# Softmax exponentials on VectorE: two bit passes and a product replaced by three shifted bit patterns, with the shifts on GpSimd

## The chip, the cores and the metric

One core of one Trainium2 chip runs the whole kernel. The metric is device time in microseconds (us). Five engines work side by side: TensorE (PE, matrix products into PSUM), VectorE (DVE), ScalarE (ACT), GpSimd (POOL) and SyncE (SP), which here issues the DMAs. Each runs its own queue of instructions in order, and semaphores tie them together. PSUM has eight banks of 128 x 512 fp32.

## The reference

Two thousand and forty-eight tokens of 640 features in bf16, 32 heads of 20 features, and a GLU of 1728 hidden features. Both halves read the same layer-normed input.

```python
x  = A_x                                          # 1 x 2048 x 640
xn = layernorm(x)
q, k, v = split_heads(xn @ A_wqkv, H=32, Dh=20)
p  = softmax((q @ k.T) * 20 ** -0.5)              # 2048 x 2048 for each head
s  = merge_heads(p @ v) @ A_wo
g  = silu((sigmoid(xn @ B_w_gate) * (xn @ B_w_up)) @ B_w_down)
out = x + s * g
```

There are 32 x 2048 x 2048 exponentials, and their number sets the scale of the kernel.

## The kernel before

**Blocks and jobs.** Heads are taken in 8 groups of 4 (`GH`), queries in 4 chunks of 512 (`QC`). A group and a chunk make a block; there are 32 (`NBLK`). In a block, a job is one head and one tile of 128 keys: a score matmul with 32 rows of contraction (line 860) writes one PSUM bank of 128 keys x 512 queries, an exponential turns it into bf16 weights, and PV matmuls (line 897) multiply the weights with the 21 columns of `vts` (one column of ones, 20 of V) and add into the block's bank `oacc`. A block has 64 jobs, the kernel 2048. Four score matmuls use the four row groups of PE side by side, four PV matmuls the four column groups. An upper bound of each query's scores is subtracted through an extra row of the operands, so that no second pass over the scores is needed.

**Two ways to an exponential.** ScalarE reads one or two banks and writes `exp` into a `pt` tile (line 80). VectorE takes the other way: line 1194 adds an offset to the scaled score and converts it to a 16-bit integer `iv`, whose bits, read as bf16, are 2 to the integer part times one plus the fraction. That is too coarse alone. So three passes over a set of four jobs (`passes`, lines 945, 948 and 951) make two slabs of `pb`: the power of two by itself, and `iv` times a mantissa correction; one PV matmul for each slab adds both into `oacc`. In `add_unit`, `k` tells which pass a PV unit came from.

**PSUM.** `scA` holds two slots of two banks for ScalarE's pairs. Three more banks, `bank[0]` to `bank[2]` (`bk` in the profile), are shared by VectorE's jobs, by all other matmul work and by a slot's third job. `oacc` is the eighth.

**The order of instructions** of PE, ScalarE and VectorE is written by a planner that runs while the program is built. It steps a clock in 0.02 us, keeps when each engine, bank and buffer comes free by assumed costs (`T_F`, `T_PV`, `T_IV`, `T_PASS`, `t_exp`), and issues the next instruction of an engine that is free. PE chooses between a fill ("F": up to two or three jobs for ScalarE and one for VectorE, lines 1279 to 1314), a round of PV ("PV") and other matmul work ("M"). Changing from one kind to another is charged `T_MODE`. A fill gives VectorE a job if a bank is free and VectorE is nearly idle (line 1283). It gives ScalarE a third job only if the bank with the slot's own number is free and not taken by that VectorE job:

```python
want = SLOT if flex[nfill % 2] <= now and d_bank != nfill % 2 else SLOT - 1
```

`claim_act` takes a head's key tiles from the front, `claim_dve` from the back. Buffers limit how far work can run ahead: three `iv`, three `pb`, three `pt` for pairs and seven for triples (`NPT, NPB, NIV`).

**Other work.** "M" items are the projections (`mk_k`, `mk_q`, `mk_ku`, `mk_qu`, `mk_v`), the GLU (`mk_gu`, `mk_down`) and the output projection (`mk_out`). They are spread over the blocks by `due()`. After a block, `norm_a` copies `oacc` out and sends its row of sums through DRAM; `norm_b`, some 6.5 us later, takes the reciprocal (line 920), broadcasts it through DRAM (line 925) and has GpSimd multiply (line 927, `on_bf`), from where SP stores into `oU` (line 935). GpSimd does little else in the middle of the kernel and is not planned there: its instructions stand in the order in which the program writes them.

Of the kernel before, what the change touches and what calls it, by code (L numbers as in the profile page):

```python
# [11 lines left out]
BF16 = mybir.dt.bfloat16  # L12
# [20 lines left out]
NPT, NPB, NIV = (3, 7), 3, 3  # L33

LOG2E = 1.4426950408889634
# [3 lines left out]
def _bits_offset():  # L39

    f = (np.arange(4096) + 0.5) / 4096
    k = float(np.mean(((1.0 + f) ** 2 / 2 + 129.0 / 128.0) / 2.0 ** f))
    return 128.0 * (127.0 - float(np.log2(k)))


B_OFF = _bits_offset()


@with_exitstack
def kernel(  # L50
# [49 lines left out]
    kTs = [persist.tile([P, S], BF16, name=f"kT{i}") for i in range(2)]  # L100
    vts = [persist.tile([P, TT, 2 * GH, VW], BF16, name=f"v{i}") for i in range(2)]
# [320 lines left out]
    T_PASS = (0.605, 0.605, 1.15)  # L422
# [8 lines left out]
    v_at = {}  # L431
    o_at = {}
# [172 lines left out]
    def mk_v(pr, tts, at):  # L605
        st = {}

        def alloc():
            st["ps"] = misc_ps()

        def mm(i, kd):
            nc.tensor.matmul(st["ps"][:, i * 2 * GC:(i + 1) * 2 * GC],  # L612
                             lhsT=xn_tok(tts[i], kd),
                             rhs=wvs[pr][:, kd, :], start=(kd == 0), stop=(kd == KD - 1))

        def done(t):
            for tt in tts:
                v_at[(pr, tt)] = t
        return Item([("PE", alloc, [(0.08, lambda i=i, kd=kd: mm(i, kd)) for i in range(len(tts)) for kd in range(KD)]),
                     ("DVE", 0.065 + 0.167 * len(tts), lambda: v_evac(st["ps"], pr, tts), "free", done)], at)  # L620
# [229 lines left out]
    def claim_dve(had):  # L850
        for b in range(base(), min(NBLK, base() + 2)):
            if q_at.get(b, 1e9) > now:
                return None
            if n_left[b] >= (D_LAST if b < NBLK - 1 else D_LAST_END):
                return take(b, max((j for j in range(GH) if left[b][j]),
                                   key=lambda j: (j not in had, len(left[b][j]), j)), -1)
        return None
# [14 lines left out]
    def add_unit(b, kt, j, src, k, ready, rel):  # L872
        if k != 0:
            pv_jobs[(b, j)] = pv_jobs.get((b, j), 0) + 1
        pv_q[j].append(dict(b=b, kt=kt, j=j, k=k, src=src, ready=ready, rel=rel))
        pv_units[b] += 1

    def pv_pick(j):
        for u in pv_q[j]:
            if u["b"] == pv_block[0] and u["ready"] <= now and v_at.get((u["b"] // NQC // 2, u["kt"]), 1e9) <= now:  # L880
                return u
        return None
# [4 lines left out]
    def pv_emit(us, end):  # L887
        for u in us:
            b, kt, j, k = u["b"], u["kt"], u["j"], u["k"]
            pr, go = divmod(b // NQC, 2)  # L890
            pv_q[j].remove(u)
            pv_units[b] -= 1
            first = not pv_started.get((b, j))
            pv_started[(b, j)] = True
            last = pv_jobs.get((b, j), 0) == TT and not any(x["b"] == b for x in pv_q[j])
            lhsT = vts[pr % 2][:, kt, go * GH + j, 0:DH + 1]
            nc.tensor.matmul(oacc[32 * j:32 * j + DH + 1, :], lhsT=lhsT, rhs=u["src"], start=first, stop=last,  # L897
                             tile_position=(0, 32 * j), skip_group_check=True)
            left, i = u["rel"]
            left[i][0] -= 1  # L900
            left[i][1] = max(left[i][1], end + PL)
# [15 lines left out]
    def norm_b(b, on, lt):  # L917
        g, c = divmod(b, NQC)
        rt = w2.tile([P, GH * QC // P], FP32, tag="rt", bufs=2, name="rt")
        nc.vector.reciprocal(out=rt, in_=lt)  # L920
        rd = dram.tile([GH, QC], FP32, name="rd", tag="rd")
        nc.sync.dma_start(out=rd.rearrange("j (i c) -> (j i) c", c=GH * QC // P), in_=rt)
        rl = w2.tile([P, QC], FP32, tag="rl", bufs=1, name="rl")
        for j in range(GH):
            nc.sync.dma_start(out=rl[32 * j:32 * j + 32, :], in_=rd[j:j + 1, :].broadcast_to((32, QC)))
        on_bf = w2.tile([P, QC], BF16, tag="on_bf", bufs=2, name="on_bf")
        nc.gpsimd.tensor_tensor(out=on_bf, in0=on, in1=rl, op=ALU.mult)  # L927
        for j in range(GH):
            f = g * GC + j * DH
            r = 32 * j + 1  # L930
            left = DH
            while left:
                t, o = divmod(f, P)
                m = min(left, P - o)
                nc.sync.dma_start(out=oU[o:o + m, t, c * QC:(c + 1) * QC], in_=on_bf[r:r + m, :])
                f += m
                r += m
                left -= m


    def passes(d, k):
        n = len(d["jobs"])
        iv, pb = d["iv"][:, 0:n, :], d["pb"][:, :, 0:n, :]
        if k == 0:
            nc.vector.tensor_scalar(out=pb[:, 0, :, :].bitcast(I16), in0=iv, scalar1=0x7F80, scalar2=1,  # L945
                                    op0=ALU.bitwise_and, op1=ALU.bitwise_or)
        elif k == 1:
            nc.vector.tensor_scalar(out=pb[:, 1, :, :].bitcast(I16), in0=iv, scalar1=0x007F, scalar2=0x3F00,  # L948
                                    op0=ALU.bitwise_and, op1=ALU.bitwise_or)
        else:  # L950
            nc.vector.tensor_tensor(out=pb[:, 1, :, :], in0=iv.bitcast(BF16), in1=pb[:, 1, :, :], op=ALU.mult)  # L951
# [86 lines left out]
    with tc.manual_schedule(engines={ENG.PE, ENG.Activation, ENG.DVE}):  # L1038
# [9 lines left out]
        free = {"PE": 0.0, "ACT": 0.0, "DVE": 0.0}  # L1048
# [6 lines left out]
        dve_pass = []  # L1055
        dve_last = None
# [30 lines left out]
        def run_item(it, eng):  # L1087
# [5 lines left out]
            if len(op) > 4:  # L1093
                op[4](end + EL)
# [4 lines left out]
        while chain or items or glu_items or any(it.i < len(it.ops) for it in active):  # L1099
# [3 lines left out]
            if bb > blk_loaded:  # L1103
                blk_loaded = bb
                g, c = divmod(bb, NQC)
                if c == 0 and g + 1 < PG:
                    spread_wst(g + 1, load_wst(g + 1))
# [25 lines left out]
            for eng in ("ACT", "DVE"):  # L1133
# [21 lines left out]
                if it is not None:  # L1155
# [3 lines left out]
                    continue  # L1159
                if eng == "ACT":  # L1160
                    s = slots[nexp % 2]
                    if nexp < nfill and s["a"] is not None and s["at"] <= now:
# [3 lines left out]
                        if buf_free(pt_left[w], NPT[w - 2]):  # L1166
                            pt = w2.tile([P, w, QC], BF16, tag=f"pt{w}", bufs=NPT[w - 2], name=f"pt{w}")
                            if m == SLOT:
                                flex[nexp % 2] = now + t_exp(1) + EL
                            if m == SLOT:  # L1170
                                exp_act(pt[:, 2, :], bank[nexp % 2])
# [11 lines left out]
                if tm is not None:  # L1183
                    timed.remove(tm)
                    norm_b(*tm[1:])
# [4 lines left out]
                pass_ok = dve_pass and (dve_pass[0]["k"] > 0 or buf_free(pb_left, NPB))  # L1190
                if iv_ok and not (dve_last == "iv" and pass_ok and now < dq[0][3] + SLACK):
                    dve_last = "iv"
# [6 lines left out]
                    d["n"] += 1  # L1199
                    if d["n"] == len(d["jobs"]) and d is not dcur:  # L1200
                        dve_pass.append(d)
                elif pass_ok:
                    dve_last = "pass"
                    d = dve_pass[0]
                    k = d["k"]
                    if k == 0:
                        d["pb"] = w2.tile([P, 2, GH, QC], BF16, tag="pb", bufs=NPB, name="pb")
                        pb_left.append([2 * len(d["jobs"]), 0.0])
                        d["rel"] = (pb_left, len(pb_left) - 1)
                    passes(d, k)  # L1210
                    d["k"] += 1
                    end = now + T_PASS[k]
                    free["DVE"] = end
                    if k != 1:
                        for x, (b, kt, j) in enumerate(d["jobs"]):
                            add_unit(b, kt, j, d["pb"][:, k // 2, x, :], k, end + EL, d["rel"])
                    if k == 2:
                        dve_pass.pop(0)
                        iv_left[d["i"]][:] = [0, end]

            if dcur is not None and claimed[0] == NJOB * NBLK:
                if dcur["n"] == len(dcur["jobs"]):
                    dve_pass.append(dcur)
# [9 lines left out]
            if free["PE"] <= now:  # L1233
# [10 lines left out]
                if cur is None:  # L1244
# [3 lines left out]
                    if m_it is None:  # L1248
                        behind = done < due() + LAG
                        for f in ((2,) if not behind and claimed[0] < NJOB * NBLK and not (FALL and not pv_ok and not can_f) else [(2, 1 - own, own), (2, own, 1 - own)][M_ORD]):  # L1250
# [18 lines left out]
                elif can_f and (margin < URGENT or (stay is None and not (flex[nfill % 2] <= now + WAIT3 and flex[nfill % 2] > now and margin > WAIT3))):  # L1269
# [9 lines left out]
                if nxt == "F":  # L1279
# [5 lines left out]
                    want = SLOT if flex[nfill % 2] <= now and d_bank != nfill % 2 else SLOT - 1  # L1285
# [11 lines left out]
                    if jobs or d_new is not None:  # L1297
                        for x, t in enumerate(jobs):
                            score_mm(scA[nfill % 2][:, x, :] if x < 2 else bank[nfill % 2], *t)
# [8 lines left out]
                        if jobs:  # L1308
                            s["a"], s["at"], s["ends"] = jobs, end + PL, 0.0
                            if len(jobs) == SLOT:  # L1310
                                flex[nfill % 2] = 1e9
# [46 lines left out]
        assert not items and not glu_items and not any(it.i < len(it.ops) for it in active)  # L1358
        for tm in timed:
            norm_b(*tm[1:])  # L1360
# [30 lines left out]
```

## Time and profile before

| | |
|---|---|
| median of 2 runs | 842.79 us (842.42 to 843.16) |
| span of the profiled execution | 839.8 us |
| around the span, against the median | 3.0 us |
| PE busy | 788.4 us, 94% |
| VectorE busy | 765.4 us, 91% |
| ScalarE busy | 796.0 us, 95% |
| GpSimd busy | 77.5 us, 9% |
| exponential jobs on VectorE / ScalarE | 471 / 1577 |
| PV matmuls from `pt` / from `pb` | 1577 / 942 |

All sums are made against the profiled execution. Busy time is the union of an engine's instructions. The granted clock of TensorE is at full speed until the last slice. The kernel has a first part of about 40 us (load, layer norm, first projections), a middle to about 803 us, in which scores are made throughout, and an end. A line of a group reads: source line, engine, operation, output <- inputs, shape and type, count | busy us, mean ns of one | idle time before it and what ended it.

### The profile page before, as it was taken

To read this page: it belongs to the slowest core of one execution; us is meant where nothing else is said; L and a number is where in the kernel's file an instruction comes from. 1 tells how busy PE (TensorE), PEld (TensorE's weight loads), DVE (VectorE), ACT (ScalarE), POOL (GpSimd) and SP (SyncE) were. 2 spreads that over 40 slices of the span, in tenths; PEclk is the share of its full clock that TensorE was granted. 3 is DMA by queue.
4 is the path that set the end of the run, shared out by engine and by line. 5 is a ranking of instruction groups with operands and counts; after the bars stand their busy time and mean duration, and the time that the engine had idled before them with its cause. 6 is when DMAs were issued, how large, how long until landed. Compare 5 with 4: busy or idle time off the path is not lost.

```text
span 839.8 us, 16932 instructions
## 1 busy us (share of the span) xinstructions
PE 788.4 (94%) x6354; PEld 278.5 (33%) x6411; DVE 765.4 (91%) x1194; ACT 796.0 (95%) x1003; POOL 77.5 (9%) x84
## 2 busy tenths in 40 slices
PE   4799999999999999999999999999999999999995
PEld 2432323333333323333333233333233322333342
DVE  7789899999899998998999999999998988999994
ACT  7799999999999999999999999999999999999970
POOL 5000000000000001000000000000000000002333
PEclk9999999999999999999999999999999999999998
DMA  5711212123222132213121232131311223111642
GB/s 154 205 51 50 60 51 49 47 57 82 72 62 63 43 85 69 68 44 82 52 61 53 68 85 67 45 92 49 109 65 46 66 71 78 28 47 57 193 147 91
DMA packets 92979, 62.21 MB, mean 74 GB/s; under 512 B 34648, under 2 KB 86408, under 8 KB 92896
## 3 DMA queue, kind: packets, MB, share of 16 engines
q1 hardware_dynamic: 92608, 60.79, 25.7%
q8 instruction: 50, 0.82, 0.4%
q10 hardware_dynamic: 288, 0.33, 0.1%
q14 instruction: 33, 0.27, 0.1%
HBM read 46.24 MB, written 12.39 MB: 70 GB/s over the span
## 4 chain that ended last, share of the span: by engine, by line
ACT 49%; PE 28%; DVE 13%; issue 6%; DMA 2%; SPq 1%; POOL 0%; POOLq 0%; ACTq 0%; DVEq 0%
ACT pt L80 44%; PE scA L860 8%; PE oacc L897 5%; DVE iv L1194 5%; PE bk L679 4%; PE bk L641 3%; ACT tnh L80 3%; DVE pb L951 2%; PE bk L765 2%; PE bk L504 2%; DVE pb L945 1%; DVE pb L948 1%; DMA ld<-on 1%; PE psk L140 1%; ACT td L80 1%
## 5 line engine op out<-in xcount | busy, mean ns | idle before, releaser
L80 ACT ACTIVATE pt<-scA 128x1024 bf16<-128x1024 f32 (+1 forms) x729 | 720.2, 1153 | 4.6 <-PE bk L860 2.9
L1194 DVE TENSOR_SCALAR iv<-bk 128x512 int16<-128x512 f32 x471 | 318.6, 682 | 31.7 <-PE bk L860 30.2
L860 PE MATMUL scA<-q,kT 32*128 32x512 bf16 x1448 | 282.6, 382 | 16.7 <-ACT pt L80 9.6
L860 PE MATMUL bk<-q,kT 32*128 32x512 bf16 x600 | 215.5, 383 | 2.0 <-DVE iv L1194 1.7
L897 PE MATMUL oacc<-pt,v 128*21 128x512 bf16 x1577 | 183.1, 382 | 0.6 <-ACT pt L80 0.3
L860 PEld LDWEIGHTS <-kT 32*128 32x128 bf16 x2048 | 88.7, 91 | 261.6 <-issue 246.8
L897 PE MATMUL oacc<-pb,v 128*21 128x512 bf16 x942 | 152.9, 382 | 1.8 <-DVE on L910 1.5
L951 DVE TENSOR_TENSOR pb<-iv,pb 128x2048 bf16<-128x2048 bf16 x118 | 146.8, 1244 | 0.8
L641 PE MATMUL bk<-xnT,wgu 128*128 128x512 bf16 x471 | 142.6, 383 | 3.6 <-issue 1.7
L927 POOL TENSOR_TENSOR on_bf<-on,rl 128x512 bf16<-128x512 f32 x30 | 43.3, 1443 | 692.7 <-DMA rl<-rd 326.0
L80 ACT ACTIVATE pt<-bk 128x512 bf16<-128x512 f32 x129 | 94.5, 733 | 4.0 <-PE bk L860 3.8
L945 DVE TENSOR_SCALAR pb<-iv 128x2048 int16<-128x2048 int16 x118 | 86.3, 731 | 2.5
L679 PE MATMUL bk<-wd,hT 128*128 128x320 bf16 x448 | 86.9, 302 | 1.2 <-DVE iv L1194 0.7
L948 DVE TENSOR_SCALAR pb<-iv 128x2048 int16<-128x2048 int16 x118 | 82.6, 700 | 0.0
L897 PEld LDWEIGHTS <-v 128*21 128x21 bf16 x2519 | 50.4, 90 | 92.2 <-issue 69.4
L641 PEld LDWEIGHTS <-wgu 128*128 128x128 bf16 x520 | 37.1, 97 | 66.2 <-issue 50.4
L679 PEld LDWEIGHTS <-hT 128*128 128x128 bf16 x448 | 34.4, 97 | 48.4 <-issue 39.4
L504 PE MATMUL bk<-xnT,wu 128*120 128x512 bf16 x160 | 49.3, 399 | 0.4 <-DVE iv L1194 0.3
L80 ACT ACTIVATE tnh<-bk 128x512 bf16<-128x512 f32 (+1 forms) x56 | 41.6, 742 | 0.1
L649 DVE SCALAR_TENSOR_TENSOR hT<-tnh,bk 128x512 bf16<-128x512 bf16 x52 | 35.3, 680 | 5.9 <-PE bk L641 5.2
L612 PE MATMUL bk<-wv,xnT 128*128 128x160 bf16 x280 | 29.2, 234 | 0.7 <-ACT pt L80 0.6
L612 PEld LDWEIGHTS <-xnT 128*128 128x128 bf16 x280 | 18.6, 98 | 14.4 <-issue 14.1
(116 smaller groups left out, 381.3 us busy)
## 6 DMA issues: line engine op xcount, KB each, us to landing
wgu<-in_B_w_gate_dram SPq DMA_DIRECT2D x24, 320.0 KB
wgu<-in_B_w_up_dram SPq DMA_DIRECT2D x24, 320.0 KB
rl<-rd SPq DMA_DIRECT2D x120, 64.0 KB
gq_dram<-gqs SPq DMA_DIRECT2D x32, 160.0 KB
xnT<-gq_dram SPq DMA_DIRECT2D x12, 320.0 KB
xt<-in_A_x_dram SPq DMA_DIRECT2D x16, 160.0 KB
wd<-in_B_w_down_dram SPq DMA_DIRECT2D x1, 2080.0 KB
oU<-on_bf SPq DMA_DIRECT2D x104, 20.0 KB
```

The lines of the kernel that those rows point to most:

```text
L80: return nc.scalar.add_instruction(mybir.InstActivation(func=func, name=nc.get_next_instruction_name(), engine=ENG.Activation, ins=[nc.sca ...
L504: nc.tensor.matmul(st["ps"][0:UC, :], lhsT=wus[u][:, kd, i, :], rhs=xnT[:, c, kd, :], start=(kd == 0), stop=(kd == KD - 1))
L612: nc.tensor.matmul(st["ps"][:, i * 2 * GC:(i + 1) * 2 * GC], lhsT=xn_tok(tts[i], kd), rhs=wvs[pr][:, kd, :], start=(kd == 0), stop=(kd == ...
L641: nc.tensor.matmul(st[key][0:fs, :], lhsT=w[:, i, kd, ko * P:ko * P + fs], rhs=xnT[:, c, kd, :], start=(kd == 0), stop=(kd == KD - 1))
L679: nc.tensor.matmul(st["ps"][:, 0:HD], lhsT=hT[0:fsz[kf], kf, t4 * P:(t4 + 1) * P], rhs=wd[0:fsz[kf], kf, h * HD:(h + 1) * HD], start=(kf = ...
L860: nc.tensor.matmul(dst, lhsT=kTs[(b // NQC) % 2][32 * j:32 * j + 32, kt * P:(kt + 1) * P], rhs=qts[b % 3][32 * j:32 * j + 32, :], start=Tr ...
L897: nc.tensor.matmul(oacc[32 * j:32 * j + DH + 1, :], lhsT=lhsT, rhs=u["src"], start=first, stop=last, tile_position=(0, 32 * j), skip_group ...
L927: nc.gpsimd.tensor_tensor(out=on_bf, in0=on, in1=rl, op=ALU.mult)
L945: nc.vector.tensor_scalar(out=pb[:, 0, :, :].bitcast(I16), in0=iv, scalar1=0x7F80, scalar2=1, op0=ALU.bitwise_and, op1=ALU.bitwise_or)
L948: nc.vector.tensor_scalar(out=pb[:, 1, :, :].bitcast(I16), in0=iv, scalar1=0x007F, scalar2=0x3F00, op0=ALU.bitwise_and, op1=ALU.bitwise_or)
L951: nc.vector.tensor_tensor(out=pb[:, 1, :, :], in0=iv.bitcast(BF16), in1=pb[:, 1, :, :], op=ALU.mult)
L1194: nc.vector.tensor_scalar(out=d["iv"][:, j, :], in0=bank[bk], scalar1=B_OFF, scalar2=0.0, op0=ALU.add, op1=ALU.max)
```

## The change

The exponential on VectorE becomes a sum of three bit patterns. `iv` itself is read as bf16 and goes straight to a PV matmul with V. Two more patterns, `iv` plus 43 and `iv` plus 85, are made by GpSimd (`shift`), each by an integer addition over a set of four jobs, and go to PV matmuls with copies of V that are scaled by 2 to the minus 43/128 and minus 85/128. The three linear interpolations have their kinks at different places, so that the ripple of their sum is small. The passes of VectorE are gone.

What follows from it: `vxs` holds the two scaled copies of V, written by GpSimd (`scale_v`) after each evacuation of V; they exist for key tiles 8 to 15 only (`KX = 8`), so `claim_dve` takes only those. There are two `pb` and two `pt` for pairs instead of three and three. A job on VectorE has three PV units, with `k` 0, 1 and 2 (`None` for ScalarE's). GpSimd is planned like the other engines: shifts, scalings and the product of the normalization (`norm_c`, 5.5 us after `norm_b` in the plan) stand in the order of their planned times. The preference between a conversion and a pass on VectorE (`SLACK`) has no more use there.

Besides, a slot's third job takes any of the three shared banks that is free, and remembers it (`s["third"]`).

```diff
-NPT, NPB, NIV = (3, 7), 3, 3
+MF = (2,)
+NPT, NPB, NIV = (2, 7), 2, 3
+KX = 8
+SHIFTS = (43, 85)
+V_SCALE = tuple(2.0 ** (-t / UNIT) for t in SHIFTS)
...
+    vxs = [[persist.tile([P, TT - KX, 2 * GH, VW], BF16, name=f"vx{k}{i}") for i in range(2)] for k in range(2)]
...
-    T_PASS = (0.605, 0.605, 1.15)
+    T_SHIFT, T_VX, T_DIV, GL = (0.15, 0.445), 0.60, 1.45, 0.25
...
             if n_left[b] >= (D_LAST if b < NBLK - 1 else D_LAST_END):
-                return take(b, max((j for j in range(GH) if left[b][j]),
-                                   key=lambda j: (j not in had, len(left[b][j]), j)), -1)
+                js = [j for j in range(GH) if left[b][j] and left[b][j][-1] >= KX]
+                if js:
+                    return take(b, max(js, key=lambda j: (j not in had, len(left[b][j]), j)), -1)
...
-            lhsT = vts[pr % 2][:, kt, go * GH + j, 0:DH + 1]
+            v, kv = (vxs[k - 1][pr % 2], kt - KX) if k else (vts[pr % 2], kt)
+            lhsT = v[:, kv, go * GH + j, 0:DH + 1]
...
-    def passes(d, k):
-        ...
+    def shift(d, k):
         n = len(d["jobs"])
+        nc.gpsimd.tensor_scalar(out=d["pb"][:, k, 0:n, :].bitcast(I16), in0=d["iv"][:, 0:n, :],
+                                scalar1=float(SHIFTS[k]), scalar2=None, op0=ALU.add)
+
+    def scale_v(pr, tts, k):
+        nc.gpsimd.tensor_scalar(out=vxs[k][pr % 2][:, tts[0] - KX:tts[-1] + 1 - KX, :, 0:1 + DH],
+                                in0=vts[pr % 2][:, tts[0]:tts[-1] + 1, :, 0:1 + DH],
+                                scalar1=V_SCALE[k], scalar2=None, op0=ALU.mult)
...
+                if eng == "POOL":
+                    ...
+                    elif pool_pass and pool_pass[0]["at"] <= now and (pool_pass[0]["k"] > 0 or buf_free(pb_left, NPB)):
+                        ...
+                        shift(d, k)
+                        end = now + T_SHIFT[0] + T_SHIFT[1] * n
+                        ...
+                            add_unit(b, kt, j, d["pb"][:, k, x, :], k + 1, end + GL, d["rel"])
...
                             if m == SLOT:
-                                flex[nexp % 2] = now + t_exp(1) + EL
-                            if m == SLOT:
-                                exp_act(pt[:, 2, :], bank[nexp % 2])
+                                flex[s["third"]] = now + t_exp(1) + EL
+                                exp_act(pt[:, 2, :], bank[s["third"]])
...
-                    norm_b(*tm[1:])
+                    args = norm_b(*tm[1:])
+                    pool_at.append((now + 5.5, T_DIV, lambda args=args: norm_c(*args)))
...
+                    iv_left[d["i"]][0] += 1
+                    add_unit(*d["jobs"][j], d["iv"][:, j, :].bitcast(BF16), 0, end + EL, (iv_left, d["i"]))
...
-                    want = SLOT if flex[nfill % 2] <= now and d_bank != nfill % 2 else SLOT - 1
+                    third = next((f for f in (0, 1, 2) if flex[f] <= now and f != d_bank), None)
+                    want = SLOT if third is not None else SLOT - 1
...
-                            score_mm(scA[nfill % 2][:, x, :] if x < 2 else bank[nfill % 2], *t)
+                            score_mm(scA[nfill % 2][:, x, :] if x < 2 else bank[third], *t)
```

## The prediction

> **What bounds the kernel now.** I read the busy shares first, then the long middle stretch alone (40 to 803 us, in which scores are made), then the costs of one step on each engine.
>
> ```profile
> PE 788.4 (94%) x6354; PEld 278.5 (33%) x6411; DVE 765.4 (91%) x1194; ACT 796.0 (95%) x1003; POOL 77.5 (9%) x84
> 40.00:803.00 763.00, 736.89 (x5959) 251.48 (x6006) 712.94 (x1084) 756.82 (x935) 51.80 (x40) 1.00 0.24 67
> ```
>
> The second line is the stretch: 763 us, then busy PE, weight loads, VectorE (DVE), ScalarE (ACT), GpSimd (POOL). ACT works 756.8 of 763 us; GpSimd 51.8. PE's figure is no measure, because a matmul's record is longer than its turn, so I count PE's turns from starts in the timeline:
>
> ```profile
> 404.36 0.39 PE L860 MATMUL scA<-q,kT 32*128 32x512 bf16 x2
> 404.69 0.58 PE L679 MATMUL bk<-wd,hT 128*128 128x320 bf16 x3
> 405.28 0.39 PE L860 MATMUL scA<-q,kT 32*128 32x512 bf16 x2
> 405.60 0.61 PE L897 MATMUL oacc<-pb,v 128*21 128x512 bf16 x6
> 406.36 0.39 PE L860 MATMUL scA<-q,kT 32*128 32x512 bf16 x2
> ```
>
> A fill of scores (up to four matmuls side by side) holds PE for 0.32 us (404.36 to 404.69). Three rounds of four PV matmuls take 0.76 (405.60 to 406.36). If every run of one kind pays the same 0.11 once, a 512-wide round is 0.213 to 0.217.
>
> ```profile
> 400.05 1.18 ACT L80 ACTIVATE pt<-scA 128x1024 bf16<-128x1024 f32 x1
> 400.95 0.60 ACT L80 ACTIVATE td<-bk 128x320 bf16<-128x320 f32 x1
> ...
> 408.65 0.57 ACT L80 ACTIVATE td<-bk 128x320 bf16<-128x320 f32 x1
> 408.97 0.74 ACT L80 ACTIVATE pt<-bk 128x512 bf16<-128x512 f32 x1
> ```
>
> ACT's turns by the same rule: 0.90 for a pair of score banks, 0.32 for a td; a single bank is 0.48 (399.57 to 400.05 in the same view). With 719 pairs, 139 singles: 647 + 67 = 714 us for 1577 exponential jobs, 0.453 each. The GLU's tanh and the rest (56 and 7 at 0.48, 32 at 0.32) are 40. Together 754: **ACT bounds the stretch, at 99%.**
>
> PE before: 729 fills x 0.32 = 233; 2519 PV matmuls, four to a round, 630 x 0.213 = 134; other matmuls by their weight loads (763 of 512 columns, 576 of 320, 280 of 160, at 0.213 and in proportion) 163 + 77 + 19 = 259; at least one switch back per fill, 729 x 0.107 = 78. Sum 704, 92% of 763. PE is second.
>
> **The change, part by part.**
>
> ```profile
> L1194 DVE TENSOR_SCALAR iv<-bk 128x512 int16<-128x512 f32 x471 | 318.6, 682 | 31.7 <-PE bk L860 30.2
> L951 DVE TENSOR_TENSOR pb<-iv,pb 128x2048 bf16<-128x2048 bf16 x117 | 145.4, 1242 | 0.8
> L945 DVE TENSOR_SCALAR pb<-iv 128x2048 int16<-128x2048 int16 x117 | 85.8, 733 | 2.5
> L948 DVE TENSOR_SCALAR pb<-iv 128x2048 int16<-128x2048 int16 x117 | 82.0, 701 | 0.0
> L126 POOL COPY wqk<-wst 128x800 bf16<-128x800 bf16 x2 | 1.9, 968 | 0.1
> L240 POOL MEMSET wqk<- 128x1280 bf16 x1 | 1.3, 1338 | 0.0
> L927 POOL TENSOR_TENSOR on_bf<-on,rl 128x512 bf16<-128x512 f32 x30 | 43.3, 1443 | 692.7 <-DMA rl<-rd 326.0
> ```
>
> (1) VectorE loses three passes per four jobs: 733 + 701 + 1242 ns by the rows, so 0.67 us a job, 118 sets, 315 us. It is not the bound, so this by itself saves nothing; it opens room for more VectorE jobs. A job then costs VectorE one row of 0.68 us instead of 1.35, and a fill lasts longer than that, so a fill can nearly always carry one. Now it is 471 jobs on 729 fills, 0.65 a fill.
>
> (2) Any free bank as third: now 129 of 729 fills have a third ACT job, since it must be the fill's own bank and the VectorE job often holds that. More thirds mean fewer fills, at 0.32 + 0.107 of PE each; ACT gains nothing from them (1.38 for three is 0.46 each).
>
> (3) I take 0.9 VectorE and 2.4 ACT jobs per fill: 2048 / 3.3 = 620 fills, 560 VectorE jobs, 1488 ACT jobs. ACT: 1488 x 0.453 + 40 = **714**, 40 less than now. The 0.9 lies between today's 0.65 and one; the 2.4 between today's 1577 / 729 = 2.16 and 3, kept low because three banks must serve the VectorE job, the third and the GLU.
>
> (4) PE: a VectorE job now has three PV matmuls instead of two. 1488 + 3 x 560 = 3168, 792 rounds, 169 us (+35). Fills 620 x 0.32 = 198 (-35), switches 66 (-12), the rest 259. Sum **692** against 704: the third bank pays for the third matmul.
>
> (5) GpSimd: two shifts of 128x2048 int16 per set, 140 sets, 280 shifts. No such row exists. From below the memset (1164 ns the faster of two, for 1280 columns) gives 1.86 us in proportion; from above the slower copy (1085 for 800, strided) 2.78. The copy is the nearest, one input and 16 bits; its faster one (852) gives 2.18, and I take 2.2: 616 us. The issue order is planned with 0.15 + 0.445 x 4 = 1.93 (541 us). Besides: 30 on_bf at 1.27 (38), 30 scalings of V of about 504 columns at the copy's rate (0.54; 16), 19 output additions at 0.9 (17): 71. Sum **687**, 612 by the plan. GpSimd has room in 735 us until a shift costs (735 - 71) / 280 = 2.37 us.
>
> The page "GPSIMD Engine Reference" of the Trainium skill (section 3.1, and the table of 4.1) speaks against moving elementwise work there: it calls VectorE about twice as fast, but names one-input work as roughly line rate. By its 1.03 cycles an element at 1.2 GHz a shift would be an estimated 1.76 us before dispatch, by its 2.6 cycles 4.4 us. The sum by the first would be 493 + 71 = 564, by the second 1232 + 71 = 1303; the memset and copy rows above lie near the first.
>
> The two engines disturb each other in this trace:
>
> ```profile
> L927 POOL TENSOR_TENSOR on_bf<-on,rl x30: 1262/1272/2170, 73.7 to 784.6; 128x512 bf16<-128x512 f32 x30
> L945 DVE TENSOR_SCALAR pb<-iv x118: 546/693/1742, 38.2 to 810.5; 128x2048 int16<-128x2048 int16 x117, 128x1536 int16<-128x1536 int16 x1
> ```
>
> (Minimum, median, maximum in ns.) on_bf grows from 1.27 to 2.17 us, and a pass from 0.69 to 1.74. The passes are what goes away; the VectorE instruction that stays at every job reads PSUM. "SBUF — State Buffer" (Who interferes with whom) explains such pairs as an exclusive lock, taken by VectorE in its two-port modes or with two SBUF inputs. By it 16 aq instructions (L547) could still each wait a shift, an estimated 16 x 2 us on an engine with slack; the sum on ACT would stay.
>
> (6) Waits and queues. on_bf goes into GpSimd's queue 5.5 us after the reciprocal. Its DMAs take about 5.0 (in the timeline the reciprocal is done at 411.25 and on_bf starts at 416.29), so it mostly finds its data; when late, shifts queue behind it, and PV behind those. On SP the 136 oU stores wait for on_bf already (61.6 us in 28 waits) and may wait two shifts more; what stands behind them there is q loaded two blocks ahead, so I cost it at nothing; without that lead a block would start up to 4.4 us late. The scalings of V sit before the block that needs them and cost nothing but GpSimd's time. A set is finished 4.4 us after its last iv instead of 2.4 (starts 0.60 + 0.60 + 1.13), covered by the pt buffers except at the end: +2. One pt pair and one pb fewer: part of the loss below.
>
> **The sum.** ACT 714, PE 692, GpSimd 612 to 687 now stand close together, so no engine will reach today's 99%; I take 97% for ACT: 714 / 0.97 = 736, 27 less than 763, and +2 at the end: -25. The profiled span is 839.8; with 3.0 outside it is the median of 842.8. Forecast **818 us**. With one job per fill on VectorE and 2.2 on ACT (640 fills) ACT falls to 687, but PE is 273 + 259 + 175 = 707; at 97% 729 (total 811), at 98% without a loss at the end 721 (800). So the forecast's own range is 800 to 826.
>
> **The rivals.**
> *PE or the banks take over.* Sums within 3% of each other rarely overlap fully. If PE gets no better than today's 92%, 692 / 0.92 = 752, total 834; with thirds that fail to come (2.16 a fill, 0.9: 669 fills) it is 286 + 259 + 172 = 717, at 94% 763, no change. For it: three banks. Against: PE's idle time now is largely ACT's doing. 835 us, chance 0.22.
> *GpSimd is too slow.* Order on PE is fixed, so a late shift stops PV, then fills, then ACT. It decides from 2.37 us a shift, and costs 28 us per 0.1 us beyond. The kernel is slower by 2% from (780 - 71) / 280 = 2.53. At 2.6: 728 + 71 = 799, +36, total 879. For it: the slower copy (2.78 in proportion), and a plan made with 1.93. Against: memset and the faster copy, and the passes that disturbed GpSimd are gone. Chance 0.24.
> *Not more jobs on VectorE.* If buffers (two pb, held through both shifts) keep it near 471, ACT keeps its 754: 843 us, chance 0.06.
>
> **How the numbers follow.** Forecast 0.48: faster by over 2%. Within 2%, about what a measurement of this kernel can tell from no change: 0.22 + 0.06 = 0.28. Slower: 0.24. The range runs from the forecast's low end, 800, up to where GpSimd at 2.56 us puts it, 868; about 0.2 is left outside, mostly above.
>
> **What would show it.** iv instructions 530 to 620 and three PV matmuls each; fills about 620 with over 250 thirds; a shift start to start at 1.9 to 2.3 us; GpSimd busy 75 to 90% of the middle; ACT still above 95% there; no rise of PE waits on pb. The forecast is wrong if iv stays near 471, if ACT drops below 92% with PE waiting for a shift, or if a shift takes over 2.4 us.

## The result and the profile after

The changed kernel takes 1507.18 us (1505.23 to 1509.13) against 842.79: the ratio is 1.789, 95% interval 1.782 to 1.797. The forecast was 818 us, with a range from 800 to 868. The busy shares of the profiled execution:

```profile
PE 1019.1 (68%) x6904; PEld 307.3 (20%) x6904; DVE 553.4 (37%) x852; ACT 828.0 (55%) x1079; POOL 1388.3 (92%) x355
```

The stretch in which scores are made now runs from 40 to about 1465 us. The columns are PE, weight loads, VectorE, ScalarE, GpSimd, then granted clock:

```profile
40.00:1465.00 1425.00, 971.12 (x6560) 281.03 (x6556) 510.59 (x755) 797.14 (x1020) 1352.58 (x310) 0.78 0.13 36
```

The last two numbers are the DMA share and GB/s. ScalarE has fallen from 99% to 56% of the stretch, and GpSimd is at 95%. It has become the bound, by one group (count | busy us, mean ns | idle before it):

```profile
L965 POOL TENSOR_SCALAR pb<-iv 128x2048 int16<-128x2048 int16 (+1 forms) x242 | 1287.8, 5345 | 67.1 <-DVE iv L1238 57.3
L85 ACT ACTIVATE pt<-scA 128x1024 bf16<-128x1024 f32 x638 | 639.8, 1034 | 164.8 <-PE bk L876 147.5
L1238 DVE TENSOR_SCALAR iv<-bk 128x512 int16<-128x512 f32 x482 | 333.8, 695 | 792.2 <-PE bk L876 776.4
L85 ACT ACTIVATE pt<-bk 128x512 bf16<-128x512 f32 x296 | 179.8, 607 | 461.4 <-PE bk L876 444.9
```

The first line is the whole result: 242 shifts of 5.35 us on average, 1288 us. The other three read as the prediction's counts: 638 fills, 296 single banks, and 482 VectorE jobs. The chain from the shift to the idle engines stands in the waits (total us, times, longest), first in the kernel before, then in the changed one:

```profile
DVE iv L1194 <- PE bk L860: 30.2, 59, 2.0
ACT pt L80 <- PE bk L860: 6.7, 11, 2.6
```

```profile
DVE iv L1238 <- PE bk L876: 776.4, 367, 13.3
ACT pt L85 <- PE bk L876: 592.4, 265, 12.7
...
PE oacc L915 <- POOL pb L965: 420.7, 163, 6.5
```

Read from the bottom: PV on PE stood 163 times for a shift, up to 6.5 us; before, PV waited for `pb` 0.3 us in all. PE's order is fixed by the program, so the fills behind that PV came late, and ScalarE and VectorE waited for scores. The granted clock of TensorE fell to 0.78 in the stretch, where it was 1.00 before. It came back to 1.00 when the waits went (first experiment of the next section), so it is read here as going with them, not as a cause; no run separates the two.

### The profile page after: what moved, and what is told of

The parts are those of the page before. It is cut to its first block, busy times and chain, and to the rows that moved or that the text cites. A ratio compares the mean times of both kernels' runs of the same rounds, so it can differ in the third digit from the quotient of the medians.

```text
span 1507.4 us, 18107 instructions
## 1 busy us (share of the span) xinstructions
PE 1019.1 (68%) x6904; PEld 307.3 (20%) x6904; DVE 553.4 (37%) x852; ACT 828.0 (55%) x1079; POOL 1388.3 (92%) x355
## 4 chain that ended last, share of the span: by engine, by line
POOL 31%; PE 9%; issue 8%; DMA 1%; DVE 1%; ACT 1%; SPq 1%; POOLq 0%; DVEq 0%; ACTq 0%
POOL pb L965 29%; PE oacc L915 2%; PE scA L876 2%; PE bk L694 1%; PE bk L780 1%; DMA rl<-rd 1%; ACT pt L85 1%; DVE iv L1238 1%; PE bk L656 1%; POOL vx L969 1%; POOL on_bf L949 1%; PE bk L511 0%; SPq L943 0%; POOL xnT L790 0%; DMA rd<-rt 0%
## 5 line engine op out<-in xcount | busy, mean ns | idle before, releaser
L965 POOL TENSOR_SCALAR pb<-iv 128x2048 int16<-128x2048 int16 (+1 forms) x242 | 1287.8, 5345 | 67.1 <-DVE iv L1238 57.3
L85 ACT ACTIVATE pt<-scA 128x1024 bf16<-128x1024 f32 x638 | 639.8, 1034 | 164.8 <-PE bk L876 147.5
L915 PE MATMUL oacc<-pb,vx 128*21 128x512 bf16 x964 | 198.5, 467 | 430.4 <-POOL pb L965 420.7
L85 ACT ACTIVATE pt<-bk 128x512 bf16<-128x512 f32 x296 | 179.8, 607 | 461.4 <-PE bk L876 444.9
L915 PE MATMUL oacc<-pt,v 128*21 128x512 bf16 x1566 | 266.6, 468 | 0.0
L876 PE MATMUL bk<-q,kT 32*128 32x512 bf16 x778 | 243.4, 465 | 18.4 <-DVE otmp L787 10.8
L656 PE MATMUL bk<-xnT,wgu 128*128 128x512 bf16 x520 | 176.4, 455 | 0.6 <-DVE iv L1238 0.2
L915 PE MATMUL oacc<-iv,v 128*21 128x512 bf16 x482 | 132.2, 443 | 4.4 <-DVE hT L664 4.2
L915 PEld LDWEIGHTS <-vx 128*21 128x21 bf16 x964 | 48.6, 94 | 333.5 <-issue 317.1
L969 POOL TENSOR_SCALAR vx<-v 128x504 bf16<-128x504 bf16 (+2 forms) x30 | 33.3, 1111 | 15.8 <-DVE v L195 14.1
```

What stands on the lines that cost most here:

```text
L85: return nc.scalar.add_instruction(mybir.InstActivation(func=func, name=nc.get_next_instruction_name(), engine=ENG.Activation, ins=[nc.sca ...
L656: nc.tensor.matmul(st[key][0:fs, :], lhsT=w[:, i, kd, ko * P:ko * P + fs], rhs=xnT[:, c, kd, :], start=(kd == 0), stop=(kd == KD - 1))
L876: nc.tensor.matmul(dst, lhsT=kTs[(b // NQC) % 2][32 * j:32 * j + 32, kt * P:(kt + 1) * P], rhs=qts[b % 3][32 * j:32 * j + 32, :], start=Tr ...
L965: nc.gpsimd.tensor_scalar(out=d["pb"][:, k, 0:n, :].bitcast(I16), in0=d["iv"][:, 0:n, :], scalar1=float(SHIFTS[k]), scalar2=None, op0=ALU.add)
L969: nc.gpsimd.tensor_scalar(out=vxs[k][pr % 2][:, tts[0] - KX:tts[-1] + 1 - KX, :, 0:1 + DH], in0=vts[pr % 2][:, tts[0]:tts[-1] + 1, :, 0:1 ...
```

## The experiments

Four theories stood against each other: the shift is dear by itself; it is dear only beside VectorE; the plan's wrong price did harm through the order; and GpSimd in the chain costs whatever its price. Beyond that it was open whether the forecast of 818 us would have held at the price that it assumed.

**The shift with its addition replaced by a copy.**

```diff
-        nc.gpsimd.tensor_scalar(out=d["pb"][:, k, 0:n, :].bitcast(I16), in0=d["iv"][:, 0:n, :],
-                                scalar1=float(SHIFTS[k]), scalar2=None, op0=ALU.add)
+        nc.gpsimd.tensor_copy(out=d["pb"][:, k, 0:n, :].bitcast(I16), in_=d["iv"][:, 0:n, :])
```

> The changed kernel with GpSimd's addition replaced by a copy of the same tile (the shift is left out, so the output is not the reference's). Everything else, the order too, is the same. Theory (price): a copy takes 2.0 to 2.3 us, which is what the prediction put in; GpSimd falls from 1388 us to 242 x 2.2 + 100 = 630; ScalarE, with 1566 jobs x 0.453 + 40 = 750, bounds again, and the time is 835 to 860. Rival (GpSimd in the chain is what costs, by its place and its latency, whatever the price): above 950.

Measured: 852.25 us, ratio to the kernel before 1.0135 (1.0115 to 1.0156). The tile's instructions (minimum, median, maximum in ns), and the stretch from 40 to 803 us:

```profile
L965 POOL COPY pb<-iv x242: 1036/1893/2358, 40.6 to 820.8; 128x2048 int16<-128x2048 int16 x120, 128x1024 int16<-128x1024 int16 x1
40.00:803.00 763.00, 736.49 (x6421) 260.28 (x6425) 468.67 (x738) 750.85 (x1002) 512.16 (x302) 1.00 0.24 65
```

With the same order, only this instruction's kind turned 1507 into 852. So the price is what cost 655 us; what GpSimd's place and the order cost besides is small, since the kernel is within 11 us of the one before. ScalarE is back at 98% (750.85 of 763). And at 1.89 us, less than the 2.2 that the prediction put in, the kernel is still 1.4% slower than before and not faster: a second error had been hidden by the first.

**GpSimd's instructions by themselves.** A kernel of its own that leaves the whole computation out. Its core:

```diff
+    rep(lambda o: ts(o, src, 43.0, ALU.add), "shA", N, I16)
...
+    rep(lambda o: ts(o, bsrc, 0.79, ALU.mult), "mulbf", N, BF16)
...
+    rep(lambda o: g.tensor_copy(out=o, in_=src), "cpi", N, I16)
...
+    rep(lambda o: g.tensor_tensor(out=o, in0=src.bitcast(I32), in1=c32, op=ALU.add), "tti", N // 2, I32)
...
+    rep(lambda o: ts(o, src, 43.0, ALU.add, 0.0, ALU.max), "sh2", N, I16)
...
+    rep(lambda o: ts(o, src, 43.0, ALU.add), "shP", N, I16, 8)
...
+    for _ in range(4):
+        ts(sh, src, 43.0, ALU.add)
```

The last loop is the group shS; `sh2` is printed as sh.

> A kernel of its own that only copies x to the output and then runs GpSimd instructions one after another on scratch tiles: the shift at 2048, 1024 and 512 columns (int16), the same instruction as a bf16 and as an fp32 product, a plain copy, an int32 addition of two tensors that holds two int16 in one element, a memset; then the shift beside VectorE conversions from PSUM, and beside VectorE passes within SBUF. Theory (the instruction is dear by itself): a shift alone takes 5.2 to 5.5 us at 2048 columns, about 2.6 ns a column, in bf16 too, and 2048 columns of a copy take 2.0 to 2.3. Rival 1 (VectorE gets in the way): alone 1.9 to 2.3 us, and 5 us only beside VectorE. Rival 2 (the integer type): int16 5.4, bf16 2.2.

Its groups on GpSimd (count | busy us, mean ns), and one line of VectorE's timeline (start, us):

```profile
L48 POOL TENSOR_SCALAR shP<-src 128x2048 int16<-128x2048 int16 x8 | 42.8, 5364 | 0.1
L48 POOL TENSOR_SCALAR sh<-src 128x2048 int16<-128x2048 int16 x4 | 28.2, 7078 | 0.1
L48 POOL TENSOR_SCALAR mulbf<-bsrc 128x2048 bf16<-128x2048 bf16 x4 | 23.0, 5756 | 0.1
L48 POOL TENSOR_SCALAR shA<-src 128x2048 int16<-128x2048 int16 x4 | 22.6, 5677 | 0.0
...
L48 POOL TENSOR_SCALAR shS<-src 128x2048 int16<-128x2048 int16 x4 | 21.4, 5362 | 0.3
L48 POOL TENSOR_SCALAR shB<-src 128x1024 int16<-128x1024 int16 x4 | 14.5, 3641 | 0.0
L64 POOL TENSOR_TENSOR ttb<-bsrc 128x2048 bf16<-128x2048 bf16 x4 | 14.3, 3591 | 0.0
L48 POOL TENSOR_SCALAR mulf<-fsrc 128x1024 f32<-128x1024 f32 x4 | 11.4, 2866 | 0.0
L63 POOL TENSOR_TENSOR tti<-src,c 128x1024 int32<-128x1024 int32 x4 | 9.2, 2330 | 0.0
...
L61 POOL COPY cpi<-src 128x2048 int16<-128x2048 int16 x4 | 7.4, 1886 | 0.0
L65 POOL MEMSET mset<- 128x2048 int16 x4 | 7.1, 1800 | 0.3 <-POOLq L101 0.3
```

```profile
28.32 44.75 DVE L48 TENSOR_SCALAR dps<-src 128x2048 int16<-128x2048 int16 x24
```

VectorE's own passes within SBUF (`dsh`, `dps`) did not run where the program writes them but from 7.8 to 73.1 us, beside shA, shB and mulbf; its conversions ran from 176.0 to 193.4, beside the first three of shP. While shS ran (219.0 to 240.7) VectorE was idle. So the instruction is dear by itself: 5.36 us, 2.6 ns a column, with VectorE idle, and the same beside conversions (shP). Beside VectorE's passes most shifts took 5.78 (shA), and the bf16 product 5.76. The type plays no part that can be told: the fp32 product of 1024 columns took 2.76 us once the passes were over (three of the four mulf), a 1024-column shift in the changed kernel 2.77. Beside the passes such a shift took 3.64 here (shB). A second operation raises the price to 7.08 (the group sh, VectorE idle). A copy is 1.89 and a memset 1.80. So this one-input arithmetic instruction (TENSOR_SCALAR) costs nearly three times a one-input copy. It is not arithmetic as such: a bf16 addition of two inputs (one tile taken twice, ttb) took 3.59.

**The plan told the true price.**

```diff
-    T_SHIFT, T_VX, T_DIV, GL = (0.15, 0.445), 0.60, 1.45, 0.25
+    T_SHIFT, T_VX, T_DIV, GL = (0.15, 1.30), 1.45, 1.45, 0.25
```

> The changed kernel with the planner told what the trace shows: a shift 0.15 + 1.30 us a job instead of 0.15 + 0.445, a scaling of V 1.45 instead of 0.60. Its order has 94 sets instead of 121. Theory (price times number): 188 shifts x 5.37 + 100 = 1110 us of GpSimd, total 1130 to 1180. Rival (a wrong plan was the damage, through an order that PE can't leave): with a right plan ScalarE bounds, (2048 - 376) x 0.453 + 40 = 797, total 880 to 920.

Measured: 1177.0 us (a single run), GpSimd busy 1099.9, 94% of its span. That is price times number (1110 expected), as the first theory has it. Knowing the price takes 330 us off 1507, and the kernel is still far above 843: the plan gives up only 27 of 121 sets, and the rest stays on GpSimd.

**One part alone: any free bank as third, in the kernel before.**

```diff
-                    want = SLOT if flex[nfill % 2] <= now and d_bank != nfill % 2 else SLOT - 1
+                    third = next((f for f in (0, 1, 2) if flex[f] <= now and f != d_bank), None)
+                    want = SLOT if third is not None else SLOT - 1
...
```

> The kernel before with one part of the change alone: any free bank serves as a slot's third. Its order has 668 fills instead of 729, and 112 sets on VectorE instead of 118. Theory: ScalarE bounds and gains nothing from triples, and loses by the VectorE jobs that find no bank: (2048 - 448) x 0.453 + 40 = 765 instead of 754, total 845 to 858. Rival (the prediction's step 2, fewer fills free PE): 61 fills x 0.43 = 26 us of PE, total 815 to 830.

Measured: 858.82 us, ratio 1.0222 (1.0194 to 1.025), just above the range of the theory and far from the rival. The VectorE jobs are 445 instead of 471:

```profile
L1193 DVE TENSOR_SCALAR iv<-bk 128x512 int16<-128x512 f32 x445 | 303.2, 683 | 66.4 <-PE bk L860 64.6
40.00:803.00 763.00, 726.68 (x5881) 251.95 (x5881) 674.72 (x1020) 757.34 (x1000) 49.31 (x38) 0.98 0.24 66
```

ScalarE is as full as before (757 of 763) and has 26 more jobs, 12 us. The rest of the 17 us is not accounted for; the granted clock of its four runs was 0.966 to 0.976, against 0.994 to 0.997 before (in the profiled run 0.64 from 740 to 760 us, 0.77 from 760 to 780 and 0.5 from 800 to 810), and what that cost is not shown. Fewer fills gained nothing.

**Both shifts on VectorE.** The plan issues them there at 0.605 us each, after the conversions. A scaling of V is planned at 1.45 us in this kernel and in those that follow.

```diff
-        nc.gpsimd.tensor_scalar(out=d["pb"][:, k, 0:n, :].bitcast(I16), in0=d["iv"][:, 0:n, :],
+        nc.vector.tensor_scalar(out=d["pb"][:, k, 0:n, :].bitcast(I16), in0=d["iv"][:, 0:n, :],
...
-                    elif pool_pass and pool_pass[0]["at"] <= now and (pool_pass[0]["k"] > 0 or buf_free(pb_left, NPB)):
-                        ...
-                        end = now + T_SHIFT[0] + T_SHIFT[1] * n
-                        free["POOL"] = end
...
+                elif pool_pass and (pool_pass[0]["k"] > 0 or buf_free(pb_left, NPB)):
+                    ...
+                    end = now + T_DSHIFT
+                    free["DVE"] = end
...
```

> The changed kernel with both shifts on VectorE instead of GpSimd, planned there at 0.605 us each (0.69 was measured for a pass of this shape). Everything else stays, the scaled copies of V and the free choice of the third bank too. Its order has 663 fills and 121 sets. Theory (with the price of the shift gone the jobs per fill are what is left of the error: 484 / 663 = 0.73 instead of 0.9): ScalarE 1564 x 0.453 + 40 = 748, time 838 to 856, no gain. Rival (the price of the shift was the whole error): VectorE's 315 us of passes become 170 and the forecast of 818 comes true, 805 to 830.

Measured: 845.1 us, ratio 1.0045 (1.0031 to 1.0059). The theory holds, the rival falls. VectorE is at 79% of the stretch and waits for scores:

```profile
L1222 DVE TENSOR_SCALAR iv<-bk 128x512 int16<-128x512 f32 x481 | 326.9, 686 | 102.1 <-PE bk L877 99.4
40.00:803.00 763.00, 739.13 (x6444) 258.75 (x6497) 602.90 (x983) 756.17 (x986) 85.01 (x70) 1.00 0.24 65
```

602.9 us of VectorE instead of 712.9, and still 481 jobs; ScalarE 756 of 763. The jobs are not held down by VectorE's time.

**A cheaper shift on GpSimd.** Two 16-bit values lie in one int32, and a tensor with the shift in both halves is added.

```diff
+    pair = const.tile([P, 2], I32, name="pair")
+    for k, t in enumerate(SHIFTS):
+        nc.vector.memset(pair[:, k:k + 1].bitcast(I16), t)
...
-        nc.gpsimd.tensor_scalar(out=d["pb"][:, k, 0:n, :].bitcast(I16), in0=d["iv"][:, 0:n, :],
-                                scalar1=float(SHIFTS[k]), scalar2=None, op0=ALU.add)
+        nc.gpsimd.tensor_tensor(out=d["pb"][:, k, 0:n, :].bitcast(I32), in0=d["iv"][:, 0:n, :].bitcast(I32),
+                                in1=pair[:, k:k + 1].broadcast_to((P, n, QC // 2)), op=ALU.add)
```

> The changed kernel with the shift on GpSimd as an int32 addition of two tensors, two 16-bit values in one element (2.33 us for 2048 values when measured by itself), planned at 2.33, a scaling of V at 1.45. Its order has 649 fills and 119 sets. Theory: GpSimd 238 x 2.33 + 100 = 655 us is off the path, ScalarE with 1572 jobs is at 752 as before: 843 to 860. Rival (GpSimd stalls PE even so, by waits that an order made ahead can't follow): 870 or more.

Measured: 851.39 us, ratio 1.0118 (1.0101 to 1.0135). The shift is 1.89 us:

```profile
L969 POOL TENSOR_TENSOR pb<-iv,pair x238: 1887/1892/2407, 42.0 to 816.1; 128x1024 int32<-128x1024 int32 x119
```

So the price that the changed kernel's plan assumed (1.93) exists, in another instruction, and the change still does not pay.

**The same with the third pattern left out** (one shift, two PV matmuls for a VectorE job).

```diff
-        if k is None or k == 2:
+        if k is None or k == 1:
...
-                            pb_left.append([2 * n, 0.0])
+                            pb_left.append([n, 0.0])
...
-                        if k == 1:
+                        if k == 0:
                             pool_pass.pop(0)
```

> The kernel of e5_packed with the third pattern left out: one shift and two PV matmuls for a VectorE job, so the output is not the reference's. Its order has 657 fills and 124 sets. Theory (the third PV matmul is what the gain is paid back to, on PE): 496 / 4 x 0.213 = 26 us of PE less, so 15 to 26 us less than e5_packed. Rival (ScalarE alone bounds): 1552 jobs x 0.453 + 40 = 743 instead of 752, at most 10 us less.

Measured: 837.04 us, 14.4 less than 851.39 (ratios to before 0.9949, 0.993 to 0.9968, and 1.0118). That lies between the two: more than ScalarE's 9 us, less than PE's 26. But the last weights came 7 us sooner, which is no more than ScalarE's share, and the rest is a shorter end (the table below). So a cost of the third PV matmul is not shown; the run also halves GpSimd's shifts and what each `pb` waits for.

**The same with the third bank bound to the slot again.**

```diff
-                    third = next((f for f in (0, 1, 2) if flex[f] <= now and f != d_bank), None)
+                    third = nfill % 2 if flex[nfill % 2] <= now and d_bank != nfill % 2 else None
```

> The kernel of e5_packed with the third job of a slot bound to the slot's own bank again, as before the change. Its order has 707 fills instead of 649, and 128 sets instead of 119. Theory (here PE is close to its bound, and fills cost it 0.43 us each): 58 fills = 25 us of PE more against 16 us of ScalarE less, so the same to 12 us more than e5_packed. Rival (the free choice costs VectorE its banks, as it did by itself): 8 to 16 us less than e5_packed.

Measured: 852.11 us, ratio 1.0134 (1.0111 to 1.0157), not to be told from 851.39. The reading is in the stretch, first of the kernel with the packed shift, then of this one:

```profile
40.00:803.00 763.00, 728.44 (x6376) 258.85 (x6433) 468.07 (x737) 755.90 (x1003) 513.35 (x301) 1.00 0.24 64
40.00:803.00 763.00, 739.95 (x6461) 254.32 (x6519) 489.34 (x770) 742.43 (x914) 543.56 (x318) 1.00 0.24 64
```

ScalarE has got its relief (742 instead of 756) and the time did not follow: the last weights came 3 us sooner, and the end took 3 us more. That fits the theory, in which the 58 fills more on PE eat it up; the rival's 8 to 16 us did not come. That PE is the bound is argued, not shown: by the prediction's own count its turns come to an estimated 724 of 763 us here, and GpSimd waited 103 us for PV to free a `pb`, against 50 in the kernel with the packed shift.

**More VectorE jobs by another constant.** Two kernels from the one with the shifts on VectorE, and one from the packed shift.

```diff
-... LEAD, LAG, D_LAST, D_LAST_END = 0.25, 4, 0.15, 0.2, 40.0, 0.0, 20, 8
+... LEAD, LAG, D_LAST, D_LAST_END = 0.25, 4, 0.15, 0.2, 40.0, 0.0, 8, 8
```

> The kernel of e3_dve with one constant changed: VectorE may claim jobs of a block until 8 are left instead of 20 (D_LAST). Its order has 126 sets instead of 121 and 657 fills instead of 663. Theory (ScalarE's number of jobs sets the time): 20 jobs x 0.453 = 9 us less than e3_dve, 834 to 839. Rival (PE has taken over, 20 more third matmuls cost it nothing less): 842 to 848, and a block's last jobs wait for their shifts.

> The kernel of e3_dve with D_LAST 14 instead of 20: 126 sets and 657 fills as in e8_dl8, with more time for a block's last shifts. Theory: 9 us less than e3_dve, 834 to 839. Rival (PE): 842 to 848. If e8_dl8 is slower than this one by over 3 us, the ends of the blocks are what costs there.

> The kernel of e5_packed, with the packed shift planned at the 1.89 us that e5_packed showed instead of 2.33, D_LAST 14 instead of 20, and bank 0 offered to other matmul work as well as bank 2. Its order has 126 sets instead of 119. Theory (ScalarE's number of jobs): 28 x 0.453 = 13 us less than e5_packed, 836 to 841. Rival (PE and the three banks): 846 to 852, no better than e5_packed.

Measured: 842.58 us, ratio 1.0009 (0.9997 to 1.0022), with `D_LAST` 8; 841.73, ratio 0.9997 (0.9983 to 1.0011), with 14; 847.74, ratio 1.0075 (1.006 to 1.0089), for the packed shift with `D_LAST` 14, bank 0 for other work and the shift planned at 1.89. The first two have 502 VectorE jobs instead of 481 and gain some 3 to 4 us on the 845.1 (0.4 to 0.5% by the ratios) where ScalarE's jobs alone would give 9. The third gains 4 of 13. No version with all three patterns beat the kernel before; the best is even with it.

**Where the gain went: the end.** A kernel ends some time after its last weights are in. The last copy of `oacc` marks that moment (start of the copy, in the profiled run of each kernel; these runs lie up to some 2 us from their medians):

| kernel | jobs on ScalarE | last copy of `oacc`, us | from there to the end, us |
|---|---|---|---|
| before | 1577 | 814.7 | 25.1 |
| shift replaced by a copy | 1566 | 822.3 | 29.1 |
| shifts on VectorE | 1567 | 813.5 | 31.6 |
| the same, `D_LAST` 8 | 1546 | 802.8 | 36.3 |
| the same, `D_LAST` 14 | 1546 | 806.2 | 33.2 |
| packed shift | 1572 | 818.7 | 30.5 |
| the same, two patterns | 1554 | 811.4 | 26.0 |
| the same, own third bank | 1539 | 815.5 | 33.5 |
| packed shift, `D_LAST` 14 | 1547 | 816.6 | 29.2 |

The lines of the kernel before, of the shifts on VectorE, and of these with `D_LAST` 14 (minimum, median, maximum in ns, first and last start):

```profile
L985 DVE COPY on<-oacc x1: 682/682/682, 814.7 to 814.7; 128x512 f32<-128x512 f32 x1
L1006 DVE COPY on<-oacc x1: 692/692/692, 813.5 to 813.5; 128x512 f32<-128x512 f32 x1
L1006 DVE COPY on<-oacc x1: 684/684/684, 806.2 to 806.2; 128x512 f32<-128x512 f32 x1
```

With the shifts on VectorE, then, ScalarE's relief did arrive: the last weights came 7 to 11 us sooner for 21 jobs fewer (9 us), as the theory has it. The end gave it back. More of the other matmul work was left over for it (145 and 128 matmuls after the last copy with `D_LAST` 8 and 14, 99 before), and the last rows of the GLU went to DRAM at 823 and 822 us (794 before), so that the final steps waited for them to be stored and loaded again. Whether PE's time or a free bank was missing earlier was not tried. With the packed shift on GpSimd the same number of jobs (1547) was done 10 us later than on VectorE (1546); there GpSimd's place in the chain seems to cost something even at 1.89 us, but that kernel also gives bank 0 to other work.

## Why the prediction was wrong

**Step 5, the price of a shift, failed: 2.2 us assumed, 5.37 measured.** I bounded it by a memset and a copy, which move data and compute nothing. That put GpSimd at 687 us, off the path; it was busy 1388 us and set the time. The on_bf product stood in the same profile with 1.26 us for 512 columns, 2.5 ns a column; in proportion that is 5.05 us for a shift, within 6%, and the prediction did not use it as a bound. That it comes so near is partly luck, since it is another instruction, with two fp32 inputs: by the experiments the kind of instruction decides (for 2048 columns a copy 1.89, a bf16 addition of two inputs 3.59, the shift 5.36). The scalings of V were priced by the copy too: 16 us in all, and they took 33, which does not matter beside the shifts.

**The rule of the page** "GPSIMD Engine Reference" of the Trainium skill (section 4.1: one-input work roughly at line rate) holds in these runs for the copy (1.89 us for 2048 columns) and not for TENSOR_SCALAR (5.36). The page gives its 2.6 cycles (section 3.1) for two inputs; the estimate by them, 4.4 us a shift, is 18% under the measured 5.37. That the sum by it, 1303 us, is close to the measured 1388 is luck: it counts 280 shifts, and there were 242.

**The rival was the right mechanism with too short a price.** "GpSimd is too slow" (chance 0.24) named the order on PE, PV waiting for a shift, and the price from which it decides, 2.37 us. It stopped at 2.6 us and 879. With the measured price and number its sum is right: 242 x 5.35 + 71 = 1366 of GpSimd, against 1388.

**Step 3, 0.9 VectorE jobs a fill, failed as well.** There were 482 on 638 fills, 0.76, and about as many when the shift cost 1.89 us or had left GpSimd (476 on 649; 481 on 663). ScalarE keeps 1566 jobs, not 1488: 78 x 0.453 = 35 us. 818 + 35 = 853 agrees with the kernel with the copy (852.25), partly by luck: with nearly the same jobs, the kernel with the shifts on VectorE took 845.1. VectorE's time was not what held the jobs down; relaxing `D_LAST` raised them by 21. The prediction's sum also took 2 us more for the end; with the shift cheap or off GpSimd, the end was 1 to 11 us longer than before. What sets the rest of the jobs (three banks, the buffers, key tiles 8 to 15 only) was not tried apart. The small rival "not more jobs on VectorE" (843, chance 0.06) describes this half; its reason, the two `pb`, was not tested.

**Step 2 and 4, the third bank pays for the third matmul:** thirds came as forecast (296 single banks, 638 fills for 620), but alone they cost 2.2% (at a lower clock), and in the changed order they brought nothing that can be measured. PE's sum had them as a gain of 47 us. One figure of the sum is a slip that nothing rests on: 1408 ScalarE jobs are 678 us, not 687.

**What held:** ScalarE's 99% before, and its 0.453 a job as a measure of when the last weights are in where the shifts were on VectorE; VectorE not the bound; on_bf's waits (none ahead of it after the change, its queue being full). **The lock of the Trainium skill's page "SBUF — State Buffer" (Who interferes with whom)** agrees with the trace: the 16 aq instructions, each with two inputs in SBUF and estimated to wait up to 2 us, took, before and after,

```profile
L547 DVE SCALAR_TENSOR_TENSOR aq<-qu x16: 678/681/1039, 167.0 to 557.3; 120x512 bf16<-120x512 bf16 x16
L554 DVE SCALAR_TENSOR_TENSOR aq<-qu x16: 692/2090/4095, 278.2 to 994.8; 120x512 bf16<-120x512 bf16 x16
```

a median of 2.09 us against 0.68, while the conversions from PSUM hardly changed (a mean of 695 ns against 682).

## What to carry to other kernels

Price an instruction that the trace lacks by a row that does the same kind of work on the same engine: here on GpSimd an arithmetic row, not a copy or a memset, and keep the dearest such row as an end of the range. Before crediting an engine's relief, ask what holds its share of the work: with both shifts on VectorE instead of the three passes, it lost 110 us of work and took ten jobs more. And read the main stretch and the end apart: ScalarE's 9 us were won in the stretch, and more than half of them was lost to work left over for the end; by the medians alone it looks as if they had never come.

## What the runs showed of the hardware

On GpSimd 2048 columns cost 1.80 us in a memset, 1.89 in a copy, 3.59 in a bf16 addition of two inputs, 5.36 in a shift of int16 and 7.08 with a second operation; an int32 addition of two tensors of 1024 elements took 2.33, and 1.89 with one element broadcast as its second input, so packing two values made the shift 2.8 times cheaper. Shifts and VectorE's passes within SBUF slow each other: beside passes most shifts took 5.78 us instead of 5.36, and a pass of 2048 int16 columns, with a median of 0.69 in the kernel before, took up to 5.84 beside shifts:

```profile
L48 DVE TENSOR_SCALAR dsh<-src x4: 2444/5838/5840, 7.8 to 21.7; 128x2048 int16<-128x2048 int16 x4
```

With PE waiting, TensorE's granted clock fell from 1.00 to 0.78 over the stretch; with the copy in the shift's place it was 1.00.
